# A routed expert guessed from 24 of 32 slots, and attention's loads in one group, in a fused attention and mixture kernel

## The chip, the core and the metric

One core of a Trainium2 chip runs the whole program. The metric is device time in microseconds (us), the median of several executions; smaller is better. Five engines work side by side, each through its own list of instructions in order: TensorE (PE, with its weight loads PEld), VectorE (DVE), ScalarE (ACT), GpSimd (POOL) and SyncE (SP), which here issues nearly all transfers (DMAs).

## The reference, cut to what matters

Attention with a position bias feeds a soft mixture of experts (every slot is a weighted mean of all tokens), and that feeds a routed mixture in which each token goes to one expert.

```python
scores = scale * np.matmul(q, k.transpose(0, 1, 3, 2)) + bias      # 4 batches, 8 heads, 576 x 576, d 64
attn = softmax(scores); x = (attn @ v) as [2304, 512]
# soft mixture: 8 experts x 4 slots
logits = x @ phi                                                   # [2304, 32]
slot_input = softmax over tokens(logits).T @ x                     # [32, 512]
slot_out[e] = np.maximum(slot_input[e] @ w1[e], 0.0) @ w2[e]       # w1 [8, 512, 1024], w2 [8, 1024, 512]
x = softmax over slots(logits) @ slot_out                          # [2304, 512]
# routed mixture
do_compute = x @ w_skip > 0
e_idx = np.argmax(x[do_compute] @ w_gate, axis=1)                  # one of 8 experts per token
out = x; out[do_compute] += gate_w * (np.maximum(x @ W1[e_idx], 0.0) @ W2[e_idx])
```

With the inputs of the reference every token is routed, and all of them to expert 0.

## The kernel before

**Bias tables.** 36 calls of `bias_batch` make the position bias: hidden units on VectorE and ScalarE (`hid`), a product on TensorE, and ScalarE's copy into one of six buffers (`ev`), which SP writes to a table in memory (`scratch`). After each eight of them SP loads one bias tile of the first pair of heads back (`bias`; the last, smaller one is `biasm`, in three pieces); such a load waits for the writes that it reads.

**Attention** runs over 16 pairs, each two heads of one batch. A pair's work is cut into named steps, and a table `SCHED` gives each step a number. The steps of all pairs are sorted by `n * II + SCHED[x]` (`II` is 14100), so that some four pairs overlap; `LAST` does this for the last four pairs. Each engine takes its steps in this written order. The numbers say in which order steps stand, and are no measurement. Steps that the prediction speaks of:

- `LK`, `LQ`, `LV`: SP loads k, q (`tk`, `tq`, 288 KB each) and v. For v there are two transfers of 64 partitions (`tn`, 224 KB each, 7 of 9 rows) and a third one for what is left (`tl`, 32 KB in rows of 256 bytes).
- `BA`, `BM`: SP loads a bias tile of the next heads (576 KB), or `biasm`.
- `KHI`, `KLO`, `QHI`, `QLO`: GpSimd splits k and q into a high and a low part (`sk`, `sq`), which frees `tk` and `tq`. `VA`: ScalarE takes `tn` and `tl` into `tv`.
- `QK..p`, `QK..e`, `EX..`: scores on TensorE, bias and row minimum on VectorE (line 469), exponential on ScalarE.
- `HI`, `LO`, `TD`: GpSimd and VectorE split the exponentials into two 16-bit halves (`ehl`), and SP issues a transposing DMA of them (`eT`, three per pair: TD0, TD1, TD2; four buffers). `AV`: TensorE multiplies `eT` by v. `AVB` does it for the leftover rows (line 589).

**Weights of the soft mixture.** 64 pieces of 512 KB: 32 of the first layer (`ph`, line 899), then 32 of the second (`pbig`, line 980), four per expert. Three pieces are loaded during attention, ten more behind the last transpose, into buffers of attention that are free by then, and `NW2` = 12 into buffers of their own (`x0` to `x11`). After that a piece is loaded whenever one has been used. The last piece comes in two halves.

**Behind the last piece** come sums over partitions (`part`, then `pc`), the gate's product `pw` (with `w10`: 8 gate columns and the skip column), `SW`, and a product with ones that adds the gate over all 32 slots; VectorE takes the largest, SP reads its index from `g_i` into a register and issues `expert_load`:

```python
        vec.tensor_scalar(out=g_i, in0=g8i[:, 0:1], scalar1=7.0, scalar2=0.0, op0=ALU.min, op1=ALU.max)
        expert_load(sync.value_load(g_i[0:1, 0:1], min_val=0, max_val=7))
```

That is 4 MB: `w1e` in four transfers, `w2e` in four. Then come 19 products for the tokens' logits (`pl`, line 1114), the transposes `p4` (line 1117), `slots(0)` with `w1e` (line 1034), and so on to the output. At the end `code` tells whether all tokens are of the guessed expert; if not, another branch loads each expert that occurs and does it all again.

## Time and profile before

| | us |
|---|---|
| median of 3 runs | 492.16 (491.25 to 494.73) |
| the profiled execution, its own time | 491.48 |
| span of the profile, first to last instruction | 489.6 |

A profile shows one execution. Busy time is the time in which an engine works on an instruction; an engine that waits for a semaphore is idle, and the profile names what came last. SP is not busy in this sense: its rows show when a DMA is issued, and how long the issue took. Engines of a stretch can all be busy for most of it and still hold each other up in turn, so the views by stage say where to look, and the waits say at what.

### The profile page before, as it was taken

To read this page: it belongs to the slowest core of one execution; us is meant where nothing else is said; L and a number is where in the kernel's file an instruction comes from. 1 tells how busy PE (TensorE), PEld (TensorE's weight loads), DVE (VectorE), ACT (ScalarE), POOL (GpSimd) and SP (SyncE) were. 2 spreads that over 40 slices of the span, in tenths; PEclk is the share of its full clock that TensorE was granted. 3 is DMA by queue.
4 is the path that set the end of the run, shared out by engine and by line. 5 is a ranking of instruction groups with operands and counts; after the bars stand their busy time and mean duration, and the time that the engine had idled before them with its cause. 6 is when DMAs were issued, how large, how long until landed. Compare 5 with 4: busy or idle time off the path is not lost.

```text
span 489.6 us, 11571 instructions
## 1 busy us (share of the span) xinstructions
PE 420.0 (86%) x4291; PEld 302.8 (62%) x4291; DVE 354.4 (72%) x824; ACT 301.7 (62%) x633; POOL 252.6 (52%) x243
## 2 busy tenths in 40 slices
PE   4786997988998989889988999998797777799983
PEld 2442466877888879879967988886363111255462
DVE  6998977976978989878988898996648100047563
ACT  4887978796886888859968879892402100027510
POOL 5630027998887899869997899772300000000000
PEclk9989998998998999989999999999989799959998
DMA  6458864999899999899999989799999999572065
GB/s 184 163 173 306 296 245 88 219 196 234 176 206 210 198 231 187 205 231 197 228 201 245 213 198 175 172 194 215 410 386 407 387 387 387 197 253 93 27 214 177
DMA packets 154076, 111.49 MB, mean 228 GB/s; under 512 B 120256, under 2 KB 126912, under 8 KB 154016
## 3 DMA queue, kind: packets, MB, share of 16 engines
q1 hardware_dynamic: 152112, 107.47, 84.8%
q10 hardware_dynamic: 1824, 2.97, 1.8%
q8 instruction: 36, 0.59, 0.5%
q0 software_dynamic: 80, 0.26, 0.2%
q14 instruction: 24, 0.20, 0.1%
HBM read 66.97 MB, written 15.34 MB: 168 GB/s over the span
## 4 chain that ended last, share of the span: by engine, by line
PE 33%; DMA 33%; DVE 16%; ACT 8%; issue 5%; POOL 3%; SPq 1%; ACTq 0%; DVEq 0%; POOLq 0%
DMA eT<-ehl 9%; PE sc L452 7%; DVE ehl L491 7%; DMA x<-in_moe_w_dram 7%; DMA bias<-in_moe_w_dram 4%; DMA scratch<-ev 4%; DVE e L469 3%; ACT ev L211 3%; PE av L589 3%; PE av L581 2%; PE sc L208 2%; PE ph L899 2%; DMA tn<-in_v_dram 2%; DMA k<-in_moe_w_dram 2%; DMA bias<-scratch 2%
## 5 line engine op out<-in xcount | busy, mean ns | idle before, releaser
L469 DVE CUSTOM_DVE_ANT_0 e<-sc,bias 128x576 f32<-128x576 f32 x128 | 95.0, 753 | 26.9 <-PE sc L452 21.2
L452 PE MATMUL sc<-k,qT 128*128 128x288 f32 x512 | 100.6, 324 | 6.0 <-DVE st L469 4.5
L476 ACT ACTIVATE e<-e,st 128x576 f32<-128x576 f32 x128 | 96.3, 778 | 4.2 <-DVE st L469 3.6
L491 DVE SCALAR_TENSOR_TENSOR ehl<-e,ehl 128x1152 f16<-128x1152 f32 x48 | 83.8, 1746 | 0.5 <-POOL ehl L487 0.4
L452 PEld LDWEIGHTS sc<-k,qT 128*128 128x128 f32 x512 | 74.8, 195 | 11.5 <-DVE st L469 7.4
L487 POOL TENSOR_SCALAR ehl<-e 128x1152 f16<-128x1152 f32 x48 | 60.2, 1262 | 7.9 <-ACT e L476 4.5
L208 PE MATMUL sc<-hid,w2b 128*32 128x288 f32 x576 | 49.9, 433 | 10.7 <-ACT ev L211 7.8
L204 DVE TENSOR_SCALAR hid<-ll,nib 128x576 f32<-128x576 f32 x117 | 55.7, 557 | 2.8 <-PE sc L208 2.8
L395 POOL TENSOR_TENSOR v<-tv,v 128x650 f16<-128x650 f32 x16 | 31.0, 1936 | 44.6 <-ACT v L391 44.6
L424 POOL TENSOR_SCALAR k<-k 64x1152 fp32r<-64x1152 f32 x30 | 51.5, 1717 | 4.6 <-ACT k L414 1.4
L581 PE MATMUL av<-v,eT 128*128 128x65 f16 x1152 | 51.3, 195 | 0.0
L208 PEld LDWEIGHTS sc<-hid,w2b 128*32 128x32 f32 x576 | 23.2, 114 | 35.2 <-ACT ev L211 20.7
L581 PEld LDWEIGHTS <-eT 128*128 128x128 f16 x1152 | 43.8, 99 | 0.9
L1106 POOL TENSOR_SCALAR Lt<-rk 128x128 f16<-128x128 f32 x1 | 0.3, 299 | 75.9 <-PE pbig L980 75.9
L211 ACT ACTIVATE ev<-sc,offs,ipi 128x576 f32<-128x576 f32 x36 | 29.9, 829 | 9.2 <-PE sc L208 5.6
L986 DVE COPY part<-pbig 128x256 f32<-128x256 f32 x1 | 0.4, 425 | 41.7 <-ACT part L985 41.7
L589 PE MATMUL av<-eq,tv 128*64 128x192 f32 x320 | 29.5, 331 | 0.0
L374 POOL TENSOR_SCALAR sk<-tk 128x576 fp32r<-128x576 f32 x16 | 18.1, 1131 | 21.8 <-DMA tk<-in_k_dram 14.5
L376 POOL TENSOR_TENSOR sq<-tq,sq 128x576 fp32r<-128x576 f32 x16 | 27.0, 1690 | 1.1
L985 ACT COPY part<-pbig 128x256 f32<-128x256 f32 x1 | 0.4, 373 | 42.6 <-PE pbig L980 42.6
L544 PE MATMUL pt<-ident,e 128*128 128x128 f32 x144 | 24.8, 285 | 0.5 <-ACT eq L549 0.5
L980 PE MATMUL pbig<-x,hT 128*32 128x512 f32 x76 | 20.5, 623 | 4.8 <-DMA x<-in_moe_w_dram 4.8
(335 smaller groups left out, 881.2 us busy)
## 6 DMA issues: line engine op xcount, KB each, us to landing
x<-in_moe_w_dram SPq DMA_DIRECT2D x30, 512.0 KB, 10.7
scratch<-ev SPq DMA_DIRECT2D x36, 288.0 KB, 4.6
bias<-scratch SPq DMA_DIRECT2D x16, 576.0 KB, 4.7
tn<-in_v_dram SPq DMA_DIRECT2D x32, 224.0 KB, 3.8
bias<-in_moe_w_dram SPq DMA_DIRECT2D x13, 512.0 KB, 10.2
k<-in_moe_w_dram SPq DMA_DIRECT2D x12, 512.0 KB
tk<-in_k_dram SPq DMA_DIRECT2D x16, 288.0 KB, 3.9
tq<-in_q_dram SPq DMA_DIRECT2D x16, 288.0 KB, 4.1
```

The source lines that it names most:

```text
L204: vec.tensor_scalar(out=hid, in0=src, scalar1=nib[:, gi:gi + 1], scalar2=None, op0=ALU.max)
L208: pe.matmul(pb[c * 32:(c + 1) * 32, hh, 0:288], lhsT=w2b, rhs=hid[:, hh * 288:(hh + 1) * 288], start=True, stop=True)
L211: act.activation(ev, pb[:, :, 0:288].rearrange("p a (l u) -> p u a l", u=NU), AF.Identity, bias=offs[not on_act], scale=ipi[:, bt:bt + 1])
L395: pool.tensor_tensor(out=z["v16"][:, 1], in0=tv, in1=z["v16"][:, 0], op=ALU.subtract)
L424: pool.tensor_scalar(out=k1[64 * i:64 * i + 64], in0=k0[64 - 64 * i:128 - 64 * i], scalar1=1.0, scalar2=1.0, op0=ALU.mult, op1=ALU.mult)
L452: pe.matmul(sc[:, hh, 0:288], lhsT=l_, rhs=kf[i][:, o:o + 288], start=(i == 0), stop=(i == 1))
L469: vec.tensor_tensor_reduce(out=z["e", t][:, o].rearrange("p (a j) -> p a j", a=2), in0=z.pop(("sc", t, j))[:, :, 0:288], in1=bias_t[hp, t] ...
L476: act.activation(ee, ee, AF.Exp, bias=z["m", t][:, j:j + 1], scale=-1.0, **kw)
L487: pool.tensor_scalar(out=eh[:, 0], in0=z["e", t], scalar1=ES, scalar2=1.0, op0=ALU.mult, op1=ALU.mult)
L491: vec.scalar_tensor_tensor(out=eh[:, 1], in0=z.pop(("e", t)), scalar=ES, in1=eh[:, 0], op0=ALU.mult, op1=ALU.subtract)
L581: pe.matmul(av[:, oj:oj + VD], lhsT=eT[:, ei, 5 * j + c], rhs=v16[:, vi, c, j], start=False, stop=lastt and k_ == 2 and c == 3)
L589: pe.matmul(z["av", 1][j * 64:(j + 1) * 64, o], lhsT=tv[:, c, j, 0:64], rhs=z["eq"][:, 4 * j + c if c < 4 else 8], start=False, stop=last ...
```

## The change

- **Tables.** `SCHED` and `LAST` have new numbers throughout. `lead`, the first load or transpose of the list, is emitted first and is held behind the last bias load (`last_bias`), so that loads written behind it don't move up into the bias tables.
- **v.** `tn` takes 8 of 9 rows in its two transfers (256 KB each), with an offset by which the two halves of partitions hold all rows between them; `tl` is gone.
- **Buffers.** `NW2` is 6, and `w1e`, `w2e` get memory of their own (`ew`) from the end of attention on.
- **The guess.** The second layer sums the first 24 pieces (experts 0 to 5) and the last 8 into separate tiles. After piece 24, `guess_a` copies the first sum out, adds it over partitions with ones, multiplies by the gate, and takes the largest; `expert_load` is issued behind the last piece. The old product with ones behind `SW` is gone. `p4` stands ahead of the logits.

```diff
-SCHED = {"LK": 0, "LQ": 172, "LV": 9234, "BA": 18742, "BM": 28658, "TD0": 29881, "TD1": 36646, "TD2": 28531,
...
+SCHED = {"LK": 0, "LQ": 6481, "LV": 18003, "BA": 29213, "BM": 40002, "TD0": 37159, "TD1": 48797, "TD2": 38491,
...
-NW2 = 12
+NW2 = 6
...
             for a in range(2) if i == 63 else (slice(0, 2),):
-                eng.dma_start(out=t2[:, a], in_=src[:, a])
+                last_piece[:] = [eng.dma_start(out=t2[:, a], in_=src[:, a])]
...
-            tn = new(v_p, [P, 2, 7, 64], F32, "tn", bufs=1)
-            tl = new(v_p, [P, 64], F32, "tl", bufs=1)
+            tn = new(v_p, [P, 2, 8, 64], F32, "tn", bufs=1)
             src = v[b, h0, 0, :]
             for a in range(2):
                 sync.dma_start(out=tn[a * 64:(a + 1) * 64].rearrange("p j u d -> p j (u d)"),
                                in_=bass.AP(tensor=src.tensor, offset=src.offset + a * 64,
-                                           ap=[[NU * 64, 64], [(S + 1) * 64, 2], [1, 448]]))
-            sync.dma_start(out=tl, in_=bass.AP(tensor=src.tensor, offset=src.offset + 512,
-                                               ap=[[S * 64 - 512, 2], [NU * 64, 64], [1, 64]]))
+                                           ap=[[NU * 64, 64], [S * 64, 2], [1, 512]]))
...
-            act.activation(tv[:, 0:4, :, 0:64], z["tn"][:, :, 0:7:2].rearrange("p j c d -> p c j d"), AF.Copy, scale=VS)
+            tn = z["tn"][:, 0, 0, :]
+            act.activation(tv[:, 0:4, :, 0:64], bass.AP(tensor=tn.tensor, offset=tn.offset,
+                                                        ap=[tn.ap[0], [2 * 64, 4], [9 * 64, 2], [1, 64]]), AF.Copy, scale=VS)
             for j in range(2):
-                r = slice(j * 64, (j + 1) * 64)
-                act.activation(tv[r, 4, j, 0:64], z["tl"][r], AF.Copy, scale=VS)
+                i, o = slice(64 - j * 64, 128 - j * 64), slice(j * 64, (j + 1) * 64)
+                act.activation(tv[o, 4, j, 0:64], z["tn"][i, j, 7 - 7 * j], AF.Copy, scale=VS)
...
+        lead = next(y for y in todo if y[2][0] == "L" and y[2][1] in "KQV" or y[2][:2] == "TD")
+        with tc.issue_after(last_bias[0].ins):
+            OPS[lead[1]][lead[2]]()
         for t_, n, x in todo:
-            OPS[n][x]()
+            if (t_, n, x) != lead:
+                OPS[n][x]()
...
+    ew = ctx.enter_context(tc.tile_pool(name="ew", bufs=1, side="right", reuse_waits="tile"))
+    w1e = ew.tile([P, 4, FF], F32, name="w1e")
+    w2e = ew.tile([P, 8, DM], F32, name="w2e")
+
+    def expert_load(ereg):
+        for a in range(4):
+            f = slice(a * 256, (a + 1) * 256)
+            sync.dma_start(out=w1e[:, :, f], in_=gw1[bass.ds(ereg, 1), :, f].rearrange("o (k p) f -> p (o k) f", p=P))
+        for a in range(4):
+            f = slice(a * 256, (a + 1) * 256)
+            sync.dma_start(out=w2e[:, 2 * a:2 * a + 2, :],
+                           in_=gw2[bass.ds(ereg, 1), f, :].rearrange("o (k p) f -> p (o k) f", p=P))
...
+        po = [p1.tile([P, DM], F32, name="pbig", bufs=2) for _ in range(2)]
+        part = [late.tile([P, DM], F32, name=f"part{i}") for i in range(2)]
+        pt = [ps.tile([P, 512], F32, name="pc") for _ in range(2)]
+        GE = 24
+
+        def half_sums(i):
+            act.copy(part[i][:, 0:256], po[i][:, 0:256])
+            vec.tensor_copy(part[i][:, 256:512], po[i][:, 256:512])
+
+        def to_T(i):
+            for kc in range(4):
+                pe.matmul(pt[kc // 2][:, kc % 2 * P:(kc % 2 + 1) * P], lhsT=part[i][:, kc * P:(kc + 1) * P], rhs=sel,
+                          start=i == 0 and kc % 2 == 0, stop=i == 1 and kc % 2 == 1)
+
+        def guess_a():
+            half_sums(0)
+            pgs = p1.tile([P, 512], F32, name="pgs")
+            for kc in range(4):
+                pe.matmul(pgs[:, kc * P:(kc + 1) * P], lhsT=part[0][:, kc * P:(kc + 1) * P], rhs=ones,
+                          start=True, stop=True)
+            gsum = sp.tile([P, 512], F32, name="gsum")
+            act.copy(gsum[:, 0:256], pgs[:, 0:256])
+            vec.tensor_copy(gsum[:, 256:512], pgs[:, 256:512])
+            pe_g = p1.tile([P, 10], F32, name="pwg")
+            for kc in range(4):
+                pe.matmul(pe_g, lhsT=gsum[:, kc * P:(kc + 1) * P], rhs=w10[:, kc, :], start=kc == 0, stop=kc == 3)
+            vec.max(out=g8, in_=pe_g[:, 0:8])
+            vec.max_index(out=g8i, in_max=g8, in_values=pe_g[:, 0:8])
+            vec.tensor_scalar(out=g_i, in0=g8i[:, 0:1], scalar1=7.0, scalar2=0.0, op0=ALU.min, op1=ALU.max)
+            with tc.issue_after(last_piece[0].ins):
+                expert_load(sync.value_load(g_i[0:1, 0:1], min_val=0, max_val=7))
+            vec.tensor_scalar(out=goff[:, 0:1], in0=g_i, scalar1=8.0, scalar2=None, op0=ALU.subtract)
+            vec.tensor_scalar(out=goff[:, 1:2], in0=g_i, scalar1=float(FF), scalar2=None, op0=ALU.mult)
+            to_T(0)
+
         for i in range(32):
             e, r = i // 4, i % 4
             for a in range(2):
                 f = 2 * r + a
                 o, g = f * 256 + e * NSL, f % 4
-                pe.matmul(po[g * 32:(g + 1) * 32, :], lhsT=hT[:, o:o + NSL],
-                          rhs=wq[32 + i][:, a * 512:(a + 1) * 512], start=(i < 2), stop=(i >= 30))
+                pe.matmul(po[i // GE][g * 32:(g + 1) * 32, :], lhsT=hT[:, o:o + NSL],
+                          rhs=wq[32 + i][:, a * 512:(a + 1) * 512], start=i % GE < 2, stop=i in (GE - 2, GE - 1, 30, 31))
             if len(wq) < 64:
                 weight_piece()
-        part = late.tile([P, DM], F32, name="part")
-        act.copy(part[:, 0:256], po[:, 0:256])
-        vec.tensor_copy(part[:, 256:512], po[:, 256:512])
-        pt = [ps.tile([P, 512], F32, name="pc") for _ in range(2)]
-        for kc in range(4):
-            pe.matmul(pt[kc // 2][:, kc % 2 * P:(kc % 2 + 1) * P], lhsT=part[:, kc * P:(kc + 1) * P], rhs=sel,
-                      start=True, stop=True)
+            if i == GE - 1:
+                guess_a()
+        half_sums(1)
+        to_T(1)
...
-        pe_g = pg.tile([P, 512], F32, name="pc")
-        pe.matmul(pe_g[:, 0:10], lhsT=onesr, rhs=SW, start=True, stop=True)
-        vec.max(out=g8, in_=pe_g[:, 0:8])
-        vec.max_index(out=g8i, in_max=g8, in_values=pe_g[:, 0:8])
-        vec.tensor_scalar(out=g_i, in0=g8i[:, 0:1], scalar1=7.0, scalar2=0.0, op0=ALU.min, op1=ALU.max)
-        expert_load(sync.value_load(g_i[0:1, 0:1], min_val=0, max_val=7))
-        vec.tensor_scalar(out=goff[:, 0:1], in0=g_i, scalar1=8.0, scalar2=None, op0=ALU.subtract)
-        vec.tensor_scalar(out=goff[:, 1:2], in0=g_i, scalar1=float(FF), scalar2=None, op0=ALU.mult)
...
+        p4 = pg.tile([P, 512], F32, name="pc")
+        for kc in range(4):
+            pe.transpose(p4[:, kc * P:(kc + 1) * P], ST4[:, kc, :], ident)
         pl = py.tile([P, 512], F32, name="y")[:, 0:NA * 10].rearrange("p (t x) -> p t x", x=10)
         for t in range(NA):
             pe.matmul(pl[:, t, :], lhsT=cT(t) if t < NT else cO, rhs=SW, start=True, stop=True)
-        p4 = pg.tile([P, 512], F32, name="pc")
-        for kc in range(4):
-            pe.transpose(p4[:, kc * P:(kc + 1) * P], ST4[:, kc, :], ident)
```

SP's list at the start, before: the first `tq` and `tl` are pair 1's, the `tk` and `tq` behind them pair 2's; `scratch<-ev` are the writes of the bias tables.

```order
L213 DMA scratch<-ev 128x576
L338 DMA tq<-in_q_dram 128x576
L350 DMA tl<-in_v_dram 128x1x64
L213 DMA scratch<-ev 128x576 x3
L333 DMA tk<-in_k_dram 128x576
L213 DMA scratch<-ev 128x576
L338 DMA tq<-in_q_dram 128x576
L213 DMA scratch<-ev 128x576 x3
L269 DMA bias_403<-scratch 128x1152
```

The same place now, up to the first bias load: the `tk` and `tq` are pair 1's.

```order
L333 DMA tk<-in_k_dram 128x576
L213 DMA scratch<-ev 128x576
L338 DMA tq<-in_q_dram 128x576
L213 DMA scratch<-ev 128x576 x7
L269 DMA bias_398<-scratch 128x1152
```

And now behind the last writes:

```order
L213 DMA scratch<-ev 128x576 x4
L272 DMA biasm<-scratch 64x576
L273 DMA biasm<-scratch 64x512
L274 DMA biasm<-scratch 64x64
L333 DMA tk<-in_k_dram 128x576
L346 DMA tn<-in_v_dram 64x2x512 x2
L338 DMA tq<-in_q_dram 128x576
L495 DMA_TRANSPOSE eT<-ehl 128x18x128 x2
```

Pair 2's k and q loads and pair 1's v loads have moved from among the first writes to behind the last piece of `biasm`.

SP's list in the middle of attention, before, a little over one pair (`eT<-ehl` are TD0 to TD2).

```order
L269 DMA bias_2420<-scratch 128x1152
L496 DMA_TRANSPOSE eT<-ehl 128x18x128
L347 DMA tn<-in_v_dram 64x2x448 x2
L350 DMA tl<-in_v_dram 128x1x64
L333 DMA tk<-in_k_dram 128x576
L338 DMA tq<-in_q_dram 128x576
L496 DMA_TRANSPOSE eT<-ehl 128x18x128 x2
L269 DMA bias_2724<-scratch 128x1152
L496 DMA_TRANSPOSE eT<-ehl 128x18x128
```

The same stretch now.

```order
L495 DMA_TRANSPOSE eT<-ehl 128x18x128 x3
L333 DMA tk<-in_k_dram 128x576
L269 DMA bias_2503<-scratch 128x1152
L346 DMA tn<-in_v_dram 64x2x512 x2
L338 DMA tq<-in_q_dram 128x576
L495 DMA_TRANSPOSE eT<-ehl 128x18x128 x3
L333 DMA tk<-in_k_dram 128x576
L269 DMA bias_2806<-scratch 128x1152
L346 DMA tn<-in_v_dram 64x2x512 x2
```

The three transposes of a period stand together and all loads ahead of them; before, a transpose stood between the bias load and the others.

TensorE's list at the end of the second layer, before: `x_6406` and `x_6410` are the last two pieces.

```order
L980 MATMUL pbig<-x_6406,hT 32x512 x2
L980 MATMUL pbig<-x_6410,hT 32x512 x2
L989 MATMUL pc<-sel,part 128x128 x4
L996 MATMUL pw<-w_6353,bias_5730 128x10 x4
L1099 MATMUL pc<-SW,onesr 128x10
L1114 MATMUL y<-SW,bias_6275 128x10 x8
L1114 MATMUL y<-SW,w 128x10 x10
L1114 MATMUL y<-SW,cO 128x10
L1117 MATMUL pc<-ident,bias_5730 128x128 x4
L1034 MATMUL pc<-w1e,bias_5730 32x256 x4
```

The stretch now in which the guess is made: `bias_6350` is the 24th piece, `k_6370` the 29th.

```order
L1030 MATMUL pbig<-bias_6350,hT 32x512 x2
L1008 MATMUL pgs<-ones,part_6328 128x128 x2
L1001 MATMUL pc<-sel,part_6328 128x128 x2
L1030 MATMUL pbig<-bias_6354,hT 32x512 x2
L1008 MATMUL pgs<-ones,part_6328 128x128 x2
L1001 MATMUL pc<-sel,part_6328 128x128 x2
L1030 MATMUL pbig<-bias_6358,hT 32x512 x2
L1030 MATMUL pbig<-bias_6362,hT 32x512 x2
L1030 MATMUL pbig<-k_6366,hT 32x512 x2
L1015 MATMUL pwg<-w_6296,gsum 128x10 x4
L1030 MATMUL pbig<-k_6370,hT 32x512 x2
L1030 MATMUL pbig<-x_6374,hT 32x512 x2
```

The sums with ones (`pgs`), with `sel` (`pc`) and with the gate (`pwg`) stand among pieces 25 to 29, and no product with ones stands behind the last piece.

## Rows read from the trace of the kernel before

**Rows 1.** Stages: us, busy of PE PEld DVE ACT POOL, granted clock, DMA share, GB/s.
```profile
0.00:66.00 66.00, 51.10 (x600) 25.25 (x600) 58.16 (x130) 51.77 (x74) 18.09 (x24) 0.97 0.68 227
...
100.00:200.00 100.00, 90.98 (x1092) 82.67 (x1091) 85.90 (x195) 80.06 (x178) 88.45 (x71) 0.97 1.02 207
200.00:300.00 100.00, 91.53 (x1070) 82.54 (x1068) 85.01 (x197) 81.50 (x183) 87.17 (x72) 0.98 1.03 209
...
339.00:424.00 85.00, 68.80 (x540) 22.68 (x539) 28.43 (x71) 12.00 (x33) 4.81 (x25) 0.94 1.02 383
424.00:490.00 66.00, 52.60 (x252) 32.89 (x250) 35.82 (x87) 21.46 (x47) 3.46 (x10) 0.87 0.44 142
```

**Rows 2.** Waits of SP's queue, 0 to 66 us: total, times, longest us.
```profile
SPq L333 <- POOL sk L376: 9.5, 2, 6.9
```

**Rows 3.** SP's queue in order of time, 26 to 34 us: start, us.
```profile
26.02 0.33 SPq L333 DMA_DIRECT2D tk<-in_k_dram  x1
26.45 0.38 SPq L213 DMA_DIRECT2D scratch<-ev  x1
28.45 0.33 SPq L338 DMA_DIRECT2D tq<-in_q_dram  x1
28.84 1.42 SPq L213 DMA_DIRECT2D scratch<-ev  x3
33.88 0.32 SPq L269 DMA_DIRECT2D bias<-scratch  x1
```

**Rows 4.** ScalarE and VectorE in order of time; in brackets idle before.
```profile
39.27 0.83 ACT L211 ACTIVATE ev<-sc,offs,ipi 128x576 f32<-128x576 f32 x1 [2.92 <-DMA scratch<-ev]
...
41.35 24.14 DVE L204 TENSOR_SCALAR hid<-ll,nib 128x576 f32<-128x576 f32 x56 [1.44 <-PE sc L208]
```

**Rows 5.** TensorE in order of time: first and fourteenth AVB.
```profile
90.99 1.85 PE L589 MATMUL av<-eq,tv 128*64 128x192 f32 x20
...
311.79 1.52 PE L589 MATMUL av<-eq,tv 128*64 128x192 f32 x16
```

**Rows 6.** Waits by engine, 100 to 300 us: total, times, longest us.
```profile
PE av L577 <- DMA eT<-ehl: 5.0, 4, 1.4
...
DVE e L469 <- DMA bias<-scratch: 4.6, 2, 2.4
...
ACT tv L384 <- DMA tn<-in_v_dram: 13.4, 8, 2.9
...
POOL sk L374 <- DMA tk<-in_k_dram: 10.0, 8, 2.0
```

**Rows 7.** Chain of waits, 194 to 216 us; landing of eT over the run.
```profile
197.76 7.35 DMA eT<-ehl
...
207.38 4.43 DMA bias<-scratch
...
DMA to landing us min/median/max: 4.6/6.0/8.0
```

**Rows 8.** Order of time around the weight stream: start, us, idle before.
```profile
358.03 1.08 PE L899 MATMUL ph<-bias,sT 128*32 128x256 f32 x8
...
419.90 1.05 PE L980 MATMUL pbig<-x,hT 128*32 128x512 f32 x4 [0.30 <-DMA x<-in_moe_w_dram]
...
421.25 1.05 PE L980 MATMUL pbig<-x,hT 128*32 128x512 f32 x4 [0.30 <-DMA x<-in_moe_w_dram]
...
425.40 1.17 PE L989 MATMUL pc<-sel,part 128*128 128x128 f32 x8 [0.46 <-ACT part L985]
...
430.40 2.20 SPq L1022 DMA_DIRECT2D w1e<-in_moe_w_dram  x4
...
433.92 1.08 PE L1034 MATMUL pc<-w1e,bias 128*32 128x256 f32 x8 [0.30 <-DMA w1e<-in_moe_w_dram]
...
436.00 1.08 PE L1034 MATMUL pc<-w1e,bias 128*32 128x256 f32 x8 [0.47 <-DMA w1e<-in_moe_w_dram]
```

**Rows 9.** The same view, one stretch behind the weight stream.
```profile
428.50:442.00 13.50, 12.73 (x64) 7.63 (x65) 6.45 (x28) 3.56 (x10) 0.40 (x1) 0.50 0.78 268
```

More of the change, by code (lines that the diff above doesn't have):

```diff
@@ L215, in bias_batch @@
                 in_=ev.rearrange("p u a l -> p (u a l)"))
-    wq = []
+    wq, last_piece = [], []
     SLOTS = ([(f"bias{i}", [P, 2 * S], F32) for i in (4,)] + [("w", [P, 1024], F32)] * 2
@@ L259, in soft_moe_attention_kernel @@
     NP = len(pairs)
-    bias_t, last_dma, X, st = {}, [], [], [dict() for _ in pairs]
+    bias_t, last_dma, last_bias, X, st = {}, [], [], [], [dict() for _ in pairs]
     xT = {}
@@ L273, in load_bias @@
             sync.dma_start(out=bt[64:128, 0:512], in_=scratch[512:576, h0 + 1, 64:S])
-            sync.dma_start(out=bt[64:128, 512:S], in_=scratch[512:576, h0 + 1, 0:64])
+            last_bias[:] = [sync.dma_start(out=bt[64:128, 512:S], in_=scratch[512:576, h0 + 1, 0:64])]
         bias_t[hp, t] = bt
@@ L962, in soft_moe_attention_kernel @@
         ones = late.tile([P, P], F32, name="ones")
-        onesr = late.tile([P, P], F32R, name="onesr")
+        g8 = late.tile([P, 8], F32, name="g8")
+        g8i = late.tile([P, 8], mybir.dt.uint32, name="g8i")
         io = late.tile([P, 2, 8], F32, name="io")
@@ L969, in soft_moe_attention_kernel @@
         pool.memset(ones, 1.0)
-        vec.tensor_copy(onesr, ones)
         for e in range(E):
@@ L1009, in soft_moe_attention_kernel @@
     py = ctx.enter_context(tc.tile_pool(name="py", bufs=4, space=PSUM, reuse_waits="tile"))
-    w1e = gw.tile([P, 4, FF], F32, name="w1e")
-    w2e = gw.tile([P, 8, DM], F32, name="w2e")
     w2h = gw.tile([P, 8, DM], F32R, name="w2h")
@@ L1017, in soft_moe_attention_kernel @@
     G = gw.tile([P, FF], F32R, name="G")
-    def expert_load(ereg):
-        for a in range(4):
-            f = slice(a * 256, (a + 1) * 256)
-            sync.dma_start(out=w1e[:, :, f], in_=gw1[bass.ds(ereg, 1), :, f].rearrange("o (k p) f -> p (o k) f", p=P))
-        for a in range(4):
-            f = slice(a * 256, (a + 1) * 256)
-            sync.dma_start(out=w2e[:, 2 * a:2 * a + 2, :],
-                           in_=gw2[bass.ds(ereg, 1), f, :].rearrange("o (k p) f -> p (o k) f", p=P))
     gs = {}
```

18 lines of the change are left out of this document (6 added, 12 removed), and 101 rows, old and new, of tables (LAST, SCHED).

## The prediction

> **What bounds the kernel now.** I read the stages first [rows 1]. The profiled execution has a span of 489.6 us inside a time of 491.48 us; the median of the three runs is 492.16, 0.7 us above it, and I carry that 0.7 through. The reader is to see four stages with different limits. Up to 66 us the bias tables are made: VectorE is busy 58.16 of 66.00 us. From 100 to 300 us attention is in its steady state, where TensorE is busy 91%, GpSimd 88%, VectorE 85%, and the DMA share is above 1. From 339 to 424 us the last 61 pieces of the expert weights stream in at 383 GB/s with a DMA share of 1.02: that stage is as long as its bytes. After 424 us a chain on TensorE ends the kernel. Then I read who waits for whom in the first two [rows 2 to 7], and the order of time around the end of the weight stream [rows 8].
>
> **Loads moved out of the bias stage.** In the old order a k load and a q load of pair 2 stand between the writes of the bias tables on SP's queue. The k load's buffer is free only when GpSimd has split pair 1's k: SP waits up to 6.9 us there [rows 2]. Behind it on SP stand the writes of finished bias tiles: the next one starts at 26.45, behind the k load at 26.02, then the q load at 28.45 stands ahead of three more, and the first bias load waits for all of them until 33.88 [rows 3]. The bias tiles have six buffers, so ScalarE stands still for 2.92 us until 39.27, and VectorE waits 1.44 us and from 41.35 works for 24.14 us without a gap [rows 4]. The new order keeps pair 1's k and q loads there and puts the rest, with the v load of pair 1, behind the last bias load. What is saved is what the engine that bounds the stage lost: **-1.4 us**. The bounds are 0 (the first bias load still waits for its eight writes) and -2.9 (ScalarE's whole stall). What is late next is the moved loads themselves: they now leave with the first transposes, a whole period of 17 us before pair 2 needs them. I cost that at nothing, covered by pair 0's and pair 1's scores; it costs a landing, some 4 us, if GpSimd runs out of work first.
>
> **Attention's order.** AVB, the product of the leftover rows, stands once in each pair; from its first one at 90.99 to its fourteenth at 311.79 are 13 periods, so 16.98 us per pair [rows 5]. TensorE is busy 182.5 of the 200 us [rows 1], 15.5 us per pair: at most 1.5 us per pair can go while the matmuls stay what they are, 21 us over 14 pairs. What the change aims at are waits for transfers: in these 200 us (11.8 pairs) TensorE waits 5.0 us for eT, VectorE 4.6 us for bias, ScalarE 13.4 us for v (tn) and GpSimd 10.0 us for k (tk) [rows 6]. The first two sit on the engines that run the scores, 9.6 us or 0.8 us per pair. The other two sit on engines with some room and reach the period only in part. In the old order the tn, tl, tk and tq loads come late, behind TD1, and the next transpose stands right behind them. One that follows them takes 7.35 us, against a least landing of 4.6, and the bias load that follows takes 4.43 more on the chain that ended last [rows 7]. In the new order all loads come ahead of three transposes in a row, so tk and tn are under way while SP issues transposes, and the transposes of TD0 and TD2 have no load right ahead of them. I take half of the direct waits, 0.4 us for each of 14 pairs, and so **-6 us**: not all, because the first transpose of the group now has more bytes ahead of it (below), and not none, because the waits of ScalarE and GpSimd also feed the rest. The bounds are -21 (TensorE never idle) and +23 (below).
>
> **v in two transfers.** One issue of 0.56 us per pair and a transfer of 32 KB go; the two tn transfers grow from 224 to 256 KB. The bytes are the same, ScalarE makes the same three copies, and SP's time is not what the period waits for once the transposes have started; 0, with 0.56 us per pair at most inside the bounds above.
>
> **The weight stream.** Six buffers of 512 KB fewer, 19 in place of 25. A piece comes every 1.35 us (419.90, 421.25), and the first product of the first layer starts at 358.03, 19 us after the stream does [rows 8]. Sixteen pieces fill 21.6 us, until about 361, and the first buffer that comes free is that of the fourth piece, some 3 us after 358.03. So I take 0, with a thin cover: what the chain from the last transpose to that product grows by beyond a microsecond or two is added one for one.
>
> **The guess and the end.** What goes on the path is one matmul and the w1e load behind it. The old kernel issues w1e at 430.40; the first w1e product stands at 433.92 after a wait of 0.30 for it and the second at 436.00 after 0.47 [rows 8]. So only about 0.8 us of the load shows now, because the 19 logit matmuls cover it: 4 MB leave the path, 0.8 us leave the time. What comes in: four sums with ones, four with sel and four with w10 among the last eight pieces, about 1.17 each [rows 8], 3.5 us together. In the stream each piece leaves TensorE 0.30 us idle [rows 8], 2.4 us for eight. The excess of 1.1 us would end behind the last piece, unless matmuls run closer when they need not wait for data. I take half of that loss, and 0.2 for the matmul that goes: 0.8 + 0.2 - 0.5 = **-0.5 us**, bounds -1.0 and +1.1. The weights should be issued about when the last piece lands, and be there 4 us later. From 428.5 to 442.0 the granted clock is 0.50, its lower level of 1.2 GHz, after a stretch in which TensorE waited on copies between few-column products [rows 9]; 12.73 us of work lie there. I leave that as it is, since that chain stays; if it ran at full clock, half of the 12.73 would go, and I count this in the low end.
>
> **Sum.** 491.5 - 1.4 - 6 - 0.5 = 483.6 for a profiled execution, and 0.7 on top: 484.3 for the median. I say 484.
>
> **Rivals.** (1) *The period stays.* Waits for transfers go but engines hand work to each other as before: VectorE and GpSimd are 85 and 88% busy, and idle time moves to another edge. For it speaks that every engine is over 80%; against it, that all four waits of [rows 6] are for transfers. Time: 492.2 - 1.9 = 490.3.
> (2) *The first transpose waits behind the whole group.* The old group ahead of a transpose is 2 x 224 + 32 + 288 + 288 = 1056 KB, at 1.35 us per 512 KB 2.8 us, and 7.35 - 4.6 is 2.75 [rows 7, 8]: the transpose waited for the loads to drain. The new group has bias in it too, 288 + 576 + 2 x 256 + 288 = 1664 KB, 4.4 us, so 9.0 in place of 7.35, 1.65 us per pair or 23 us over 14 pairs if AV needs that tile at once. It decides when TD1, now first, has less than that to spare; with half of it covered the time is 490.3 + 11.5 = 502. Against it: TD0 and TD2 get a clear queue, and the old order paid a toll of that kind too, on TD2. The Trainium skill (DMA: Bandwidth & Descriptors, section Queues, rings and completion order) has the same rule: on each engine's ring descriptors are consumed in order. By that rule a group of loads is a toll on the first transpose and not on the two others; the trace agrees, 2.75 against 2.8.
> (3) *The period falls to near TensorE's work*, by 1.0 of the 1.5 us: 490.3 - 14 = 476.
> (4) *The guess is wrong*, and the slow branch reloads the weights. Worked out from the inputs, the gate's sums over 24 slots are 0.0123 for expert 0 and 0.0040 for the next, and all tokens go to expert 0, so this needs other inputs; it would add at least what follows the load now, 59 us.
>
> **How the numbers follow.** Forecast 484 (480 to 488) 0.42; (1) 0.25; (2) 0.14; (3) 0.16; (4) 0.01; the last 0.02 is a planner's order that stalls elsewhere by over 5 us. About 1%, 4.9 us, is what a measurement here can tell from no change: the forecast is faster in nearly all of its range (below 487.2), (3) in all, (1) in none; so faster 0.57, same 0.27, slower 0.16. The range runs from 474, past (3) with a little of the clock's gain, to 498, inside (2).
>
> **What the new profile would show.** No standstill of ScalarE near 36 us, and VectorE at its gapless stretch 1 to 3 us earlier. In attention, waits for tk and tn near nothing and AVB about 16.5 us apart; for (1) the period stays at 17 with waits on engines; for (2) TensorE waits for eT of TD1 by a microsecond or more in every pair; for (3) the period is under 16. The weight stream stays 85 us long without a gap, w1e is issued near its end, and the first w1e product follows the logits with no wait. It would be wrong if the replanned tables stall VectorE on scores more than the loads ever did, which the trace of before cannot show.

## The result

The changed kernel takes 482.19 us (median of 4 runs, 481.06 to 484.54), the kernel before 493.45 on the same chip (491.25 to 496.04): a ratio of 0.975 (95% interval 0.970 to 0.979), 11.3 us. Predicted were 484 us, 474 to 498. The profiled execution took 484.54 us, the longest of the four, with a span of 482.8; the span before was 489.6. The sum came out; its terms did not, as this and the next sections show. Some executions fall into a slower state of the chip, and all medians and ratios below leave those out.

The changed kernel by stages: stretch in us, then busy time of PE, PEld, DVE, ACT and POOL, granted clock, DMA share, GB/s.

```profile
0.00:66.00 66.00, 55.25 (x607) 30.43 (x608) 58.51 (x131) 52.05 (x74) 18.00 (x24) 0.97 0.66 219
100.00:200.00 100.00, 93.67 (x1120) 85.10 (x1119) 85.26 (x204) 84.22 (x187) 88.21 (x74) 0.98 1.07 214
200.00:300.00 100.00, 91.46 (x1054) 80.75 (x1054) 83.82 (x196) 80.72 (x179) 86.50 (x71) 0.98 1.01 208
336.50:421.50 85.00, 69.08 (x584) 28.32 (x585) 29.21 (x75) 13.72 (x37) 4.96 (x25) 0.96 1.01 385
421.50:482.80 61.30, 49.45 (x251) 30.40 (x250) 34.84 (x81) 21.38 (x47) 3.19 (x9) 0.92 0.47 153
```

The reader is to see that attention and the weight stream look as in [rows 1], and that the piece behind the stream is nearly 5 us shorter (there 424 to 490, here 421.5 to 482.8).

**Bias stage.** SP's queue of the changed kernel: start, duration of the issue (us).

```profile
14.97 12.72 SPq L213 DMA_DIRECT2D scratch<-ev  x7
29.61 0.32 SPq L269 DMA_DIRECT2D bias<-scratch  x1
...
72.14 0.60 SPq L274 DMA_DIRECT2D biasm<-scratch  x1
```

ScalarE and VectorE there, in order of time, with idle time before in brackets, and last VectorE's wait for `biasm` in the kernel before:

```profile
36.34 0.82 ACT L211 ACTIVATE ev<-sc,offs,ipi 128x576 f32<-128x576 f32 x1
...
25.34 38.61 DVE L204 TENSOR_SCALAR hid<-ll,nib 128x576 f32<-128x576 f32 x85 [1.36 <-PE sc L208]
...
74.64 0.76 DVE L468 CUSTOM_DVE_ANT_0 em<-sc,biasm 128x576 f32<-128x576 f32 x1 [3.20 <-DMA biasm<-scratch]
```

```profile
76.35 0.76 DVE L469 CUSTOM_DVE_ANT_0 em<-sc,biasm 128x576 f32<-128x576 f32 x1 [3.37 <-DMA biasm<-scratch]
```

From 14.97 us to the first bias load no k, q or v load stands among the writes any more; that bias load is issued at 29.61, 4.3 us earlier than in [rows 3]. ScalarE has no standstill near 36 us, and VectorE's gapless stretch ends at 63.95 in place of 65.49 [rows 4], 1.5 us earlier, where I had forecast 1.4. That VectorE then waits 3.20 us for `biasm`, and waited 3.37 us before, is what I had not looked for: the last bias load, and not VectorE's stretch, releases the next step. It matters below.

**Attention.** TensorE of the changed kernel, first and fourteenth AVB:

```profile
91.69 1.85 PE L588 MATMUL av<-eq,tv 128*64 128x192 f32 x20
...
307.25 1.85 PE L588 MATMUL av<-eq,tv 128*64 128x192 f32 x20
```

That is 16.58 us per pair, against 16.98 [rows 5]; the forecast was about 16.5. The waits from 100 to 300 us (total, times, longest us):

```profile
POOL ehl L486 <- ACT e L475: 20.0, 10, 3.1
...
DVE e L468 <- PE sc L451: 12.6, 14, 1.6
...
PE av L576 <- DMA eT<-ehl: 10.7, 8, 2.7
```

The waits for tk, tn and bias of [rows 6] are gone; TensorE's wait for eT has doubled from 5.0. The chain of waits from 190 to 216 us, and below it the landing of eT over the run:

```profile
195.11 6.33 DMA eT<-ehl
...
204.21 9.54 DMA eT<-ehl
```

```profile
DMA to landing us min/median/max: 4.5/5.3/9.5
```

The median of 6.0 in [rows 7] can't be set against the 5.3 here: the trace of before has the landing of only 15 of its 48 transposes, this one has all. The run e11 below has the old tables and all 48 landings, with a median of 5.5 and a longest of 8.1. By place in a pair (pairs 1 to 13), TD1 behind the group of loads has a median of 6.65 us here, TD0 and TD2 behind it 5.27 and 4.65; in e11 it is 5.84 for TD2 behind its loads, 4.68 for TD0 and 5.29 for TD1 behind a bias load. Three transposes together take about as long in either order (16.6 and 15.8; 16.1 and 16.2 over all 16 pairs): the toll was gathered on one of them.

**Behind the stream.** TensorE of the changed kernel around the last piece, SP's issue of the expert's weights, and two stretches of the stages; last, most of the logits of the kernel before:

```profile
356.28 0.64 PE L915 MATMUL ph<-bias,sT 128*32 128x256 f32 x8 [0.23 <-DVE sT L905]
...
420.16 2.32 PE L1030 MATMUL pbig<-x,hT 128*32 128x512 f32 x8 [0.20 <-DMA x<-in_moe_w_dram]
422.95 1.17 PE L1001 MATMUL pc<-sel,part 128*128 128x128 f32 x8 [0.46 <-ACT part L996]
...
425.77 1.06 PE L1143 MATMUL y<-SW,bias 128*128 128x10 f32 x8
426.68 1.26 PE L1143 MATMUL y<-SW,w 128*128 128x10 f32 x10
...
427.98 0.64 PE L1070 MATMUL pc<-w1e,bias 128*32 128x256 f32 x8
```

```profile
420.39 2.13 SPq L833 DMA_DIRECT2D w1e<-in_moe_w_dram  x4
```

```profile
424.50:428.50 4.00, 3.97 (x38) 3.35 (x37) 0.72 (x5) 0.75 (x2) 0.44 (x4) 1.00 1.00 317
428.50:435.40 6.90, 5.92 (x35) 2.45 (x31) 4.79 (x20) 2.93 (x8) 0.40 (x1) 0.51 0.74 283
```

```profile
428.45 1.85 PE L1114 MATMUL y<-SW,bias 128*128 128x10 f32 x8
430.16 2.27 PE L1114 MATMUL y<-SW,w 128*128 128x10 f32 x10
```

`w1e` is issued about as the last piece lands, and its first product follows the logits without a wait. (SP had by then waited 6.9 us for the guess: here the guess, and not the last piece, times the issue.) From the first sum behind the last piece (422.95) to that product are 5.03 us, against 8.52 [rows 8]. The logits run at a granted clock of 1.00 and take 2.3 us in place of 4.2, and the stretch near 0.50 is 6.9 us long instead of 13.5 [rows 9].

### The profile page after: what moved, and what is told of

Read it like the earlier page. It is cut to its first block, busy times and chain, and to the rows that moved or that the text cites. A ratio compares the mean times of both kernels' runs of the same rounds, so it can differ in the third digit from the quotient of the medians.

```text
span 482.8 us, 11572 instructions
## 1 busy us (share of the span) xinstructions
PE 419.8 (87%) x4314; PEld 309.0 (64%) x4314; DVE 349.5 (72%) x825; ACT 304.9 (63%) x635; POOL 248.0 (51%) x243
## 4 chain that ended last, share of the span: by engine, by line
PE 43%; DMA 30%; DVE 7%; ACT 7%; POOL 6%; issue 4%; SPq 1%; ACTq 0%; POOLq 0%; DVEq 0%
DMA eT<-ehl 16%; PE sc L451 8%; PE sc L208 8%; DMA x<-in_moe_w_dram 6%; PE av L580 4%; DMA k<-in_moe_w_dram 2%; DMA bias<-in_moe_w_dram 2%; DVE ehl L490 2%; PE pt L406 2%; DVE xnat L1306 2%; ACT ev L211 2%; POOL k L423 2%; PE av L576 2%; PE pbig L1030 2%; PE pt L686 2%
## 5 line engine op out<-in xcount | busy, mean ns | idle before, releaser
L468 DVE CUSTOM_DVE_ANT_0 e<-sc,bias 128x576 f32<-128x576 f32 x128 | 92.5, 750 | 19.1 <-PE sc L451 18.7
L451 PE MATMUL sc<-k,qT 128*128 128x288 f32 x512 | 97.5, 321 | 7.0 <-DVE st L468 4.8
L486 POOL TENSOR_SCALAR ehl<-e 128x1152 f16<-128x1152 f32 x48 | 63.7, 1331 | 71.1 <-ACT e L475 68.4
L208 PE MATMUL sc<-hid,w2b 128*32 128x288 f32 x576 | 52.5, 434 | 6.5 <-ACT ev L211 3.7
L423 POOL TENSOR_SCALAR k<-k 64x1152 fp32r<-64x1152 f32 x30 | 47.2, 1575 | 3.8 <-ACT k L439 1.8
L208 PEld LDWEIGHTS sc<-hid,w2b 128*32 128x32 f32 x576 | 27.5, 114 | 29.4 <-ACT ev L211 12.8
L371 POOL TENSOR_SCALAR sk<-tk 128x576 fp32r<-128x576 f32 x16 | 30.4, 1899 | 10.4 <-PE pt L434 4.8
L588 PE MATMUL av<-eq,tv 128*64 128x192 f32 x320 | 29.5, 331 | 0.0
L576 PE MATMUL av<-v,eT 128*128 128x130 f16 x144 | 16.5, 224 | 14.3 <-DMA eT<-ehl 14.3
L543 PE MATMUL pt<-ident,e 128*128 128x128 f32 x144 | 24.4, 281 | 2.0 <-ACT e L475 2.0
L588 PEld LDWEIGHTS av<-eq,tv 128*64 128x64 f32 x320 | 21.6, 137 | 3.7 <-issue 0.5
L548 ACT COPY eq<-pt 128x512 f32<-128x512 f32 x32 | 18.7, 586 | 8.0 <-PE pt L543 7.6
```

The source lines that it names most:

```text
L208: pe.matmul(pb[c * 32:(c + 1) * 32, hh, 0:288], lhsT=w2b, rhs=hid[:, hh * 288:(hh + 1) * 288], start=True, stop=True)
L371: pool.tensor_scalar(out=sx[:, :, 0, :], in0=t, scalar1=1.0, scalar2=1.0, op0=ALU.mult, op1=ALU.mult)
L423: pool.tensor_scalar(out=k1[64 * i:64 * i + 64], in0=k0[64 - 64 * i:128 - 64 * i], scalar1=1.0, scalar2=1.0, op0=ALU.mult, op1=ALU.mult)
L451: pe.matmul(sc[:, hh, 0:288], lhsT=l_, rhs=kf[i][:, o:o + 288], start=(i == 0), stop=(i == 1))
L468: vec.tensor_tensor_reduce(out=z["e", t][:, o].rearrange("p (a j) -> p a j", a=2), in0=z.pop(("sc", t, j))[:, :, 0:288], in1=bias_t[hp, t] ...
L486: pool.tensor_scalar(out=eh[:, 0], in0=z["e", t], scalar1=ES, scalar2=1.0, op0=ALU.mult, op1=ALU.mult)
```

## The marks of all runs

Every kernel was also profiled once. These marks are the starts of the first bias load, of the third `biasm` load and of the last transpose's issue, the end of the second layer's last product, and the end of the span (us); behind them the three differences, which I call attention, stream and end.

| run | bias load | biasm | last transpose | last piece | end | attention | stream | end part |
|---|---|---|---|---|---|---|---|---|
| before | 33.9 | 74.0 | 335.2 | 424.9 | 489.6 | 261.2 | 89.7 | 64.7 |
| changed | 29.6 | 72.1 | 333.1 | 422.5 | 482.8 | 261.0 | 89.4 | 60.3 |
| e1_hold | 29.5 | 71.6 | 334.5 | 425.0 | 490.4 | 262.9 | 90.4 | 65.4 |
| e2_tail | 33.5 | 76.9 | 341.5 | 430.8 | 490.2 | 264.6 | 89.3 | 59.4 |
| e3_attn | 30.1 | 72.7 | 332.8 | 423.0 | 486.9 | 260.1 | 90.2 | 63.9 |
| e4_nohold | 36.0 | 78.9 | 337.4 | 426.9 | 488.3 | 258.5 | 89.4 | 61.4 |
| e5_ev9 | 34.4 | 76.7 | 338.2 | 427.7 | 492.2 | 261.5 | 89.5 | 64.5 |
| e6_td1 | 28.7 | 72.0 | 339.4 | 431.6 | 491.2 | 267.4 | 92.2 | 59.6 |
| e7_lateload | 28.8 | 71.3 | 331.6 | 422.3 | 486.5 | 260.3 | 90.6 | 64.2 |
| e8_noguess | 29.6 | 71.6 | 332.9 | 426.8 | 486.9 | 261.3 | 93.9 | 60.2 |
| e9_again | 32.9 | 75.9 | 338.1 | 427.5 | 488.1 | 262.2 | 89.4 | 60.6 |
| e10_cover | 29.1 | 71.7 | 333.7 | 422.1 | 482.6 | 262.0 | 88.4 | 60.5 |
| e11_oldtab | 29.6 | 72.8 | 336.0 | 426.3 | 487.0 | 263.2 | 90.2 | 60.8 |
| e12_oldv | 29.4 | 72.6 | 333.8 | 422.7 | 482.1 | 261.2 | 88.9 | 59.4 |

Single executions scatter, so I compare groups of them, and use the timed ratios beside. The executions of e2 and e9 began late, for a reason given at the end.

## The experiments

The first four ran on one chip (before there: 495.68 us), the next four on a second (494.83), the last four on a third (495.92). Ratios are to before on the same chip, with 95% intervals.

### The parts apart: e1, e2, e3, e4

e1 is the kernel before plus the hold alone; e2 is before plus the guess, its buffers and the end (`NW2`, `ew`, `guess_a`, `p4`); e3 is the changed kernel with the end as before; e4 is the changed kernel without the hold:

```diff
-        lead = next(y for y in todo if y[2][0] == "L" and y[2][1] in "KQV" or y[2][:2] == "TD")
-        with tc.issue_after(last_bias[0].ins):
-            OPS[lead[1]][lead[2]]()
         for t_, n, x in todo:
-            if (t_, n, x) != lead:
-                OPS[n][x]()
+            OPS[n][x]()
```

> The kernel before, with one part of the change alone: the loads that used to move up into the bias tables are held behind the last bias load. My forecast gave this part -1.4 us (bounds 0 and -2.9). By the trace of the changed kernel VectorE reached its first scores 1.5 us earlier, so 490.5 to 492.5 against a median before of 492 to 494. Rival: the loads that now leave with the first transposes cost attention as much as the bias stage gains, and the time is the same within 0.5 us.

> The kernel before, with the guess from 24 slots, the expert's weights behind the last piece, six weight buffers in place of twelve, and the transposes ahead of the logits; attention and bias stage as before. The forecast gave -0.5 us (bounds -1.0 and +1.1). Rival, from the two traces: the piece from the first copy behind the last weight piece to the first product with the expert's weights went from 8.95 to 5.46 us, and the rest of the kernel gave about 1 us more, so -3.5 to -4.5 us. If -4 is measured, the tail term was mis-sized; if it is within 1 us, the 3.5 us in the trace belong to attention, by way of the clock.

> The changed kernel with the guess, the expert's load, the weight buffers and the end as before: hold, new tables and v in two transfers alone. By the forecast -1.4 and -6, so -7.4 us. By the two traces the last transpose is issued 2.0 us earlier, so -2 to -3. By the measured medians (-11.3 in all) less a tail of -4 it would be -7. A time of -10 or more would say that the tail is worth nothing.

> The changed kernel without the hold, so that the loads of pair 2 and the v load of pair 1 move up among the bias writes again. If the hold is worth the 1.4 to 1.5 us of the bias stage here too, the changed kernel is 1.4 to 2 us faster than this one. If attention absorbs it (its end came only 2.0 us earlier in all), the two agree within 0.5 us.

Measured: e1 490.74 us, 0.990 (0.987 to 0.993), so about -5 us for the hold alone, more than three times the forecast and beyond its bound of -2.9. e2 492.12 us, 0.995 (0.991 to 0.999), -2.5 us with an interval from -0.7 to -4.4, between the forecast and the rival; by the marks its end part is 59.4 in place of 63.9 to 65.4 us. e3 489.19 us, 0.986 (0.982 to 0.991), -6.8; over the hold, tables and v together bring 1.9, which the two intervals don't tell from nothing. e4 490.07 us, 0.988 (0.982 to 0.994): without the hold the changed kernel loses a third to a half of its gain. SP's queue in e4 shows how:

```profile
26.01 0.33 SPq L333 DMA_DIRECT2D tk<-in_k_dram  x1
26.39 1.27 SPq L346 DMA_DIRECT2D tn<-in_v_dram  x2
27.75 0.54 SPq L213 DMA_DIRECT2D scratch<-ev  x1
28.39 0.38 SPq L338 DMA_DIRECT2D tq<-in_q_dram  x1
28.86 2.39 SPq L213 DMA_DIRECT2D scratch<-ev  x3
36.00 0.32 SPq L269 DMA_DIRECT2D bias<-scratch  x1
```

The k load waits for GpSimd until 26.01, writes stand behind it, the first bias load leaves at 36.00, and the last one at 78.89, 6.8 us later than in the changed kernel. From the first write to the first bias load it is 20.5 to 22.9 us in the three runs without the hold that began in time (before, e4, e5), and 15.4 to 17.0 in the ten runs with it. The last bias load lies at 74.0 to 78.9 in those three (mean 76.5) and at 71.3 to 72.8 in nine of the ten (mean 72.0). With the two late starters, e2 without the hold and e9 with it, the means are 76.6 and 72.4. The profiled execution of before happened to be the mildest case.

Where GpSimd loses the time shows in its own rows, the first half of pair 1's k split in the kernel before and in e9:

```profile
17.33 7.18 POOL L374 TENSOR_SCALAR sk<-tk 128x576 fp32r<-128x576 f32 x1 [4.84 <-PE pt L435]
```

```profile
21.30 0.77 POOL L371 TENSOR_SCALAR sk<-tk 128x576 fp32r<-128x576 f32 x1 [3.23 <-PE pt L434]
```

In twelve profiles it takes 7.17 or 7.18 us and ends some 0.5 us after VectorE's gapless stretch (at 24.51 and 23.98 in the kernel before). In e2 and e9 it starts 0.3 to 0.4 us behind a pause of VectorE and takes 0.67 and 0.77. So in that stretch the split seems to wait for VectorE; spans on GpSimd are rough, and no run here tested it.

### Which resource carried the delay: e5

In e4 ScalarE stood still for 3.8 us on a full set of buffers, and TensorE's clock was at 0.50 right behind it. So my theory was that this standstill and the clock made the 5 us.

```diff
-        ev_ = bctx.enter_context(tc.tile_pool(name="bev", bufs=6, side="right"))
+        ev_ = bctx.enter_context(tc.tile_pool(name="bev", bufs=9, side="right"))
```

> The kernel before with nine buffers for finished bias tiles in place of six and nothing else; the loads of pair 2 still stand among the bias writes. Theory: the hold is worth 5 us and not 1.4, because ScalarE's standstill on a full set of buffers is followed in most executions by a stretch at the lower TensorE clock inside the bias tables, which the profiled execution of before happened not to have. Three more buffers let ScalarE run on through the standstill (3.8 us, about 1.4 us per buffer), so most of the hold's gain should come without the hold: 490 to 492.5 against a median before of about 495, no wait of ScalarE for buffers and the last bias load at 71 to 73 us. Rival: the hold gains by what it does to attention's loads, or SP's queue itself is what delays the stage; then this is the same as before, and the last bias load stays at 74 us or later.

Measured: 493.18 us, 0.997 (0.993 to 1.001). The theory fell, its rival stands. VectorE and SP's queue in e5:

```profile
25.65 38.51 DVE L204 TENSOR_SCALAR hid<-ll,nib 128x576 f32<-128x576 f32 x85 [1.49 <-PE sc L208]
...
79.14 0.76 DVE L469 CUSTOM_DVE_ANT_0 em<-sc,biasm 128x576 f32<-128x576 f32 x1 [7.55 <-DMA biasm<-scratch]
```

```profile
34.36 0.32 SPq L269 DMA_DIRECT2D bias<-scratch  x1
...
76.70 0.60 SPq L274 DMA_DIRECT2D biasm<-scratch  x1
```

With nine buffers the standstill is gone and VectorE's stretch is as in the changed kernel, but the bias loads are as late as ever, and VectorE pays at the end: it waits 7.55 us for `biasm` in place of 3.20. From the first bias load to the third `biasm` load is 42.3 us here, 42.5 in the changed kernel, 42.9 in e4: a chain of writes and loads on SP's queue that keeps the lag it starts with. In thirteen of the fourteen profiles it lies between 42.0 and 43.4; in the profiled execution of before it was 40.1, so some 2.4 us had been made up.

### The toll on the first transpose: e6

```diff
-"TD1": 48797,
+"TD1": 45000,
```

> The changed kernel with the first transpose of the group moved ahead of the v and q loads (one number of the table), so that 864 KB stand ahead of it and 800 KB ahead of the second. Rival 2 of the prediction has the group of 1664 KB as a toll on the first transpose; its landing went to a median of 6.65 us against 4.65 to 5.27 for the other two, and TensorE waits 10.7 us for eT in 200 us. If that toll sets the period, the waits fall to about half and the time by 3 to 6 us. If the loads only have to be somewhere and the toll moves on to the second transpose, the time is the same within 2 us.

Measured: 491.90 us, 0.994 (0.991 to 0.997), slower than the changed kernel (0.975 and, as e9, 0.982); attention takes 267.4 us in place of 261. The waits from 100 to 300 us:

```profile
DVE e L468 <- PE sc L451: 26.6, 15, 4.6
ACT tv L382 <- DMA tn<-in_v_dram: 11.7, 7, 2.4
...
PE av L576 <- DMA eT<-ehl: 5.9, 6, 1.5
```

TensorE's waits for eT fell to about half, as I expected for the case that the toll sets the period, and the kernel got slower all the same: ScalarE waits for v again, VectorE twice as long for scores, and the period is 17.01 us, as long as with the old tables. The toll is there, but early loads are worth more.

### The end: e7 and e8

In e7 the load of the expert's weights takes its index behind SW:

```diff
-            with tc.issue_after(last_piece[0].ins):
-                expert_load(sync.value_load(g_i[0:1, 0:1], min_val=0, max_val=7))
...
+        vec.scalar_tensor_tensor(out=g_l, in0=SW[:, 0:1].bitcast(F32), scalar=0.0, in1=g8i[:, 0:1], op0=ALU.mult, op1=ALU.add)
+        expert_load(sync.value_load(g_l[0:1, 0:1], min_val=0, max_val=7))
```

> The changed kernel with the expert's weights issued only after SW, where the old kernel issued them; the early guess and the order of the products as in the changed kernel. The forecast held that the logit products cover that load but for 0.8 us: then +0.8. Theory from the traces: in the old kernel the logits took 4.2 us at the lower clock and hid the load; at full clock they take 2.3 us, and the load shows: w1e issued about 5.4 us behind the last piece in place of 2 us ahead of it, landing some 4 us later, so the first product with w1e 3 to 4 us later and the time 3 to 4 us longer than the changed kernel's, 485 to 487 where that has 482.

Measured: 485.65 us, 0.979 (0.974 to 0.984); the interval overlaps the changed kernel's, on another chip, and so the timing shows no loss for certain. The trace has to decide. SP's issue and the first products with w1e:

```profile
426.79 2.47 SPq L833 DMA_DIRECT2D w1e<-in_moe_w_dram  x4
```

```profile
430.40 1.08 PE L1071 MATMUL pc<-w1e,bias 128*32 128x256 f32 x8 [1.76 <-DMA w1e<-in_moe_w_dram]
...
433.86 1.08 PE L1071 MATMUL pc<-w1e,bias 128*32 128x256 f32 x8 [1.85 <-DMA w1e<-in_moe_w_dram]
```

Two waits for w1e of 1.76 and 1.85 us, and an end part of 64.2 us, where the nine other new ends lie between 59.4 and 61.4: of the 4.4 us between old ends (mean 64.6) and new ones (mean 60.2), this one step takes back 4.0 in this execution.

In e8 the guess is not computed:

```diff
-            half_sums(0)
-            pgs = p1.tile([P, 512], F32, name="pgs")
...
+            vec.tensor_scalar(out=g_i, in0=ones[:, 0:1], scalar1=0.0, scalar2=None, op0=ALU.mult)
...
-        GE = 24
+        GE = 32
```

> The changed kernel with the guess left out: expert 0 is taken without computing it, and the second layer is summed in one tile again, so the eight products with ones and with sel for the first half, the four with the gate and their copies are gone from the last eight pieces. The forecast put 3.5 us of products against 2.4 us of idle time there and took half of the excess, 0.5 us (at most 1.1). Theory from the trace: TensorE is not behind at the last piece (it waits 0.20 us for it), so the guess costs nothing and the time is the changed kernel's within 0.5 us. If the products keep the clock up, this one is slower by 1 us or more.

Measured: 489.88 us, 0.990 (0.985 to 0.994), slower. But not at the end, where TensorE waits 0.19 us for the last piece and the end part is 60.2 us: the guess costs nothing there. What is longer is the stream, 93.9 us. TensorE's first product of the first layer in e8, the stage ahead of it, and below them what SP's queue waits for there, 340 to 372 us (total, times, longest), in e8, in the changed kernel, and in e10 with ten buffers:

```profile
359.24 1.08 PE L915 MATMUL ph<-bias,sT 128*32 128x256 f32 x8
```

```profile
333.00:362.00 29.00, 24.30 (x214) 14.13 (x214) 15.25 (x49) 7.94 (x22) 4.66 (x24) 0.84 0.98 325
```

```profile
SPq L239 <- PE ph L915: 9.3, 8, 6.8
```

```profile
SPq L239 <- PE ph L915: 4.1, 6, 2.2
```

```profile
SPq L239 <- PE ph L916: 1.3, 5, 0.3
```

In this execution the granted clock averaged 0.84 on the chain from the last transpose to that product, which came 26.3 us behind the transpose and not 23.2; all buffers were full, SP waited 6.8 us for the first one to be used, and no piece landed for 4.35 us. In the changed kernel it waited 2.2 us. The longest such wait is 2.0 to 4.2 us in the other runs with six buffers and at most 1.6 in the four with twelve, so six are already fewer than the chain needs. The code up to there is the changed kernel's, and one profile doesn't tell whether all six runs (486.7 to 493.0) lost it there: why e8 is slower in the median stays open.

### The yardstick, the cover, the tables, v: e9 to e12

e9 is the changed kernel itself. e10 has ten buffers: `w2e` moves back to the memory that it had before and is loaded from there. e11 has the old `SCHED` and `LAST`, e12 the old three transfers of v.

```diff
-NW2 = 6
+NW2 = 10
...
-    w2e = ew.tile([P, 8, DM], F32, name="w2e")
...
+    w2e = gw.tile([P, 8, DM], F32, name="w2e")
+    expert_load2(eregs[0])
```

> The changed kernel itself, unchanged, as the yardstick for the three others on this chip. Its ratio to before was 0.9747 (0.9703 to 0.9792); the same is expected here, 482 to 484 where before has 495. If it comes out near 0.985, part of the differences seen so far against single parts belong to the chip and not to the parts.

> The changed kernel with ten weight buffers of their own in place of six: the second half of the expert's weights (w2e) goes back into memory that attention and the weight pieces have held, and is loaded behind w1e as before. The forecast gave the six buffers 0 with a thin cover. In the runs with six buffers the stream has a gap of up to 4.35 us some 30 us after the last transpose, and the last product of the second layer stands 89.3 to 93.9 us behind the last transpose; with twelve it was 89.5 to 90.4 without such a gap. If the cover is what varies, this kernel has no gap over 1.6 us there and is 1 to 4 us faster than the changed kernel in the median. If six buffers are enough, the two agree within 0.5 us.

> The changed kernel with the old tables of numbers; hold, v in two transfers, guess and end as in the changed kernel. The forecast gave the tables -6 us, from half of the waits for transfers. By the spacing of the products of the leftover rows the period fell from 16.98 to 16.58 us, but the last transpose came only 2.0 us earlier, and the hold is worth more of that than thought. So by the forecast this kernel is 6 us slower than the changed one; by the traces (fill and drain of the longer pipeline take back what the shorter period gives) 1 to 3 us slower.

> The changed kernel with v in three transfers again, the small one in rows of 256 bytes. The forecast gave this part 0, at most 0.56 us per pair, 9 us in all, if SP's issuing bounds the period. In the changed kernel SP issues transposes for 10 to 11.6 us of a period and loads for 2.8 us more, so that there is little room: theory, it is worth 0 to 3 us (this kernel slower); rival, nothing, within 0.5 us.

Measured: e9 487.44 us, 0.982 (0.977 to 0.988), so some 0.7 per cent of a ratio can lie between one group of runs and another, and small differences may only be read within one of these groups. (Its profiled execution is one of its slower ones, 489.93 us.) e10 483.19 us, 0.974 (0.969 to 0.979), the best here, with runs from 482.06 to 485.32 where e9 has 485.15 to 490.27. By the marks its stream is 88.4 us, 1.0 less than e9's; another 4 us between the two profiles lie at the very start of e9, so the cover is worth 1 us in the trace and up to 4 in the median. e11 488.23 us, 0.985 (0.979 to 0.990): the old tables are 0.8 us slower than e9, which the intervals don't tell from nothing. e12 484.03 us, 0.976 (0.970 to 0.981): the old three transfers of v came out 3.4 us faster than e9, with overlapping intervals, so v in two shows no gain.

## Why the prediction was right in sum and wrong in its terms

| term | forecast, us | by the marks, us |
|---|---|---|
| hold | -1.4 (0 to -2.9) | -4.5 (76.5 to 72.0, without e2 and e9; e1 timed -5) |
| tables, v | -6 (-21 to +23) | -1.9 (262.7, five runs, to 260.8, eight runs without e6) |
| stream | 0 | +0.4 (90.0, four runs, to 90.4, nine runs) |
| guess, end | -0.5 (-1.0 to +1.1) | -4.4 (64.6 to 60.2; e2 timed -2.5) |
| sum | -7.9 | -10.4 (timed -11.3, and -8.5 as e9) |

That the sum fell into the range is luck: hold and end together gave some 7 us more than forecast, and tables and v some 4 us less.

**Hold.** The step that failed is "what is saved is what the engine that bounds the stage lost". I priced the loads by VectorE's stretch, but the stage ends with the last bias load, and SP's queue carries its lag there (e4, e5). In the two profiles of before and after the price even seems right, 1.5 us in VectorE's stretch and 1.8 in the last bias load, because the execution of before had made up 2.4 us on the way; over the runs it is 4.5 to 5. The sign stood in the rows that I had: the first bias load at 33.88 [rows 3], 4.3 us later than now. The Trainium skill (DMA: Bandwidth & Descriptors, section Queues, rings and completion order) has each DMA engine consume descriptors in ring order; the order that cost here lies one step earlier, in the list of the issuing engine, where a k load that waited for GpSimd held finished tiles back. That the moved loads cost nothing held: in e1 attention is as long as in the others with the old tables.

**Attention.** The period fell as forecast, 16.98 to 16.58, and waits for tk and tn went. The step that failed is taking 0.4 us "for each of 14 pairs" as the stage's gain. In the new order AVB stands later: from the third `biasm` load to the first AVB it is 19.6 us (72.14 to 91.69) against 17.0, and from the fourteenth to the last transpose 25.9 against 23.4. Filling and draining take back 5.0 of the 5.2 us in these two profiles; over all profiles 1.9 us remain. They agree without exception: the period is 16.93 to 17.24 us in the five with the old tables and 16.41 to 16.66 in the eight with the new ones (e6 aside), the filling 17.0 to 18.4 and 18.6 to 20.0, the draining 23.2 to 24.4 and 25.9 to 27.0. The timing alone (e3 over e1, e11 beside e9) doesn't tell the remainder from nothing. Rival 1 is the nearest in size, but for another reason than it gave. Rival 2's toll exists, 6.65 against 4.65 to 5.27 us, and TensorE waits 0.9 us per pair for it; e6 shows that trading it away costs more. The median is not the 9.0 that I worked out, because I built on a single landing of 7.35: the landings at that place that the trace of before has go from 5.6 to 8.0.

**v.** 0 is not contradicted, and more than that the timing of e12 can't show.

**Stream.** "A thin cover" was right: where the first product came 23.2 us behind the last transpose, SP waited 2.2 us for a buffer and the stream lost little; at 26.3 us it waited 6.8 and the stream stood still (e8), 4.5 us longer for 3.1 us of chain and so somewhat more than one for one; with ten buffers it waits 0.3 (e10).

**Guess and end.** Two steps failed. "Only about 0.8 us of the load shows now, because the 19 logit matmuls cover it": they covered it because they ran near the lower clock, 4.2 us in place of 2.3; in e3, with the old end, they ran in 2.3 us, and the first w1e product still came 9.6 us behind the last piece (9.0 in before), after a wait of 2.89 us:

```profile
432.60 1.08 PE L1037 MATMUL pc<-w1e,bias 128*32 128x256 f32 x8 [2.89 <-DMA w1e<-in_moe_w_dram]
```

The load was the bound, and work at the lower clock hid it (e7's trace: 4.0 of 4.4 us). And the 1.1 us excess of the guess's products did not appear: the last piece finds TensorE waiting, 0.20 us (0.19 without the guess, e8).
